# First batch of a windowed attention in blocks of 64 queries by 96 keys, with a joint softmax for its last 64 tokens

## The chip, the cores and the metric

The kernel runs on one core of one Trainium2 chip. The metric is the time of one execution on the device in microseconds (us). Before the change the median of three runs is 910.67 us (910.56 to 910.86).

## What is computed

Attention over 8 batches of 8 heads, 576 tokens, 64 elements a head, in fp32; heads 0 to 3 look back over 32 tokens, heads 4 to 7 over every fourth of the last 128. The result, as 4608 tokens of 512 elements, goes through two dense layers with a clamped square between them.

```python
scores = q @ k.T / 8                       # per batch and head, 576 x 576
rel = pos[:, None] - pos[None, :]
mask_plain = (rel >= 0) & (rel < 32)                       # heads 0 to 3
mask_dil = (rel >= 0) & (rel < 128) & (rel % 4 == 0)       # heads 4 to 7
attn = exp(where(mask, scores, -1e9) - max)
attn = attn / (attn.sum(-1) + 1e-09)
x = (attn @ v), heads side by side         # 4608 x 512
h = x @ w_in                               # 512 x 2048
g = where(h >= 1, h, where(h <= -1, 0, (h + 1) ** 2 / 4))
out = g @ w_out                            # 2048 x 512
```

The weights arrive as 64-bit floating-point words and are made into pairs of fp32r tiles (a high and a low part) on the chip.

## The kernel before, in words

**The dense layers.** The 4608 tokens form 9 tiles of 512, the 2048 hidden elements 16 blocks of 128: 144 steps, named by `s`. In a step `layer1` (line 658) adds up 12 products of 128x128 by 128x512 in the bank `h0` or `h1` (`A s.c` in the order below, three products for each chunk `c` of 128 input elements: high weight by `xh`, low weight by `xh`, high weight by `xl`). Then come `clamped` (VectorE, `y`), `squared` (ScalarE, `s`), `activated` (VectorE, `j`), `g_high` (ScalarE, `g`), `g_low` (VectorE, `d`), and `layer2` (`B s.m`, 12 products for the four blocks `m` of 128 tokens, in the banks `acc0` to `acc3`, through all 16 steps of a tile). A bank `h` is free for the step after next when `g_low` has read it.

**Attention.** Heads are numbered through all batches, 0 to 63. For a head, queries are cut into 6 tiles of 96, each with a stretch of 128 keys that reaches 32 back; for heads 4 to 7 the tokens are sorted by their remainder by 4, so that every fourth token becomes a neighbour. Heads 0 to 15 (two batches, `n < native`) have their scores made directly in fp32 (`scores`, line 309, one product of 64x96 by 64x128 for a tile, two heads of a pair in turn from the upper and the lower 64 partitions); a product in fp32 shows as two records in the trace, a transpose and a product of the dense layers as one. The steps of a head and their letters: `S` scores (TensorE), `r` scale, mask and minimum in one VectorE instruction (line 288), `e` exponential (ScalarE, line 386 for one tile with the sum beside it, line 383 for a whole head, after `z`, GpSimd's subtraction of the minimum, with `u`, VectorE's sum, behind it), `i` and `R` the inverse of the sum (VectorE), `n` the product with it (GpSimd, or VectorE for heads in `by_vector`), `T` six transposes (TensorE, line 470), `p` copies of the turned weights to SBUF (line 476, ScalarE or VectorE by `kept_by_vector`), `V` the product with the values (line 540, in two parts of three tiles for a pair of heads), `x` and `l` the high and the low part of x (ScalarE line 576, VectorE line 581). As a token tile holds 512 tokens and a batch 576, x of a pair is written in three or four pieces.

**The order.** Up to step 17 every engine's order is written out by hand: `OPENING` (line 46) is a list of such letters with the head or the step behind them, played from left to right; each engine takes its instructions in that order. `W` is a number of spin products on a constant that nobody reads; seven more stand ahead of the first scores. `q`, `k`, `v`, `wi`, `wo` are loads, all on SP's queue; `a`, `b`, `j`, `h`, `l` with a weight's name are the five steps that convert a weight block (ScalarE, ScalarE, VectorE, ScalarE or GpSimd, GpSimd). Since SBUF is full, the first batch's queries, keys, values and weights lie in the places of weight blocks that are loaded later (`home`), and its turned weights in the places of the third token tile's x (`first_pts`). From step 18 on a plain loop sets TensorE's and SP's order and a planner the rest.

The opening thus works off the first batch's eight heads, starts the dense layers as soon as x of the first 512 tokens is there, and lays the second batch's heads (8 to 15) among the steps of token tile 0.

Of the kernel before, what the change touches and what calls it, by code (L numbers as in the profile page):

```python
# [49 lines left out]
e3.5 S4.3 R1 S5.3 T0.1 n1 r4.3 e3.0 r4.0 e2 r4.1 r4.2 r5.3 r5.1 e3.2 r5.0 u2 e3.1 W6 S6.0 bwi0 S7.0 S6.1 S7.1  # L50
i3 S6.2 r5.2 S7.2 e4.3 S6.3 R3 S7.3 i2 jwi0 S6.4 e4.2 n3 S7.4 S6.5 S7.5 e4.0 r6.3 r6.0 e4.1 r6.1 e6.3 r6.2
r7.3 W3 S4.4 e6.1 r7.2 r7.1 e6.2 hwi0 r7.0 R2 e6.0 r6.4 S5.4 S4.5 r6.5 S5.5 e6.4 r7.5 T3.0 wi9 r7.4 e6.5 r4.5
n2 T1.0 v2 r4.4 e5.2 p3.0 T1.1 e4.4 wi4 i6 p1.0 r5.5 wi2 R6 r5.4 e4.5 n6 p1.1 q8 W2 T3.1 e5.0 p0.1 T2.0 e5.3
i4 k10 p3.1 V0.0 e5.5 R4 p2.0 wi5 e5.1 T2.1 n4 e5.4 T6.0 wi3 p2.1 x0.0.0 V0.1 u5 wo2 e7.3 e7.0 wi6 l0.0.0
x0.1.0 lwi0 x0.1.1 e7.1 i5 l0.1.0 W2 V2.0 e7.2 R5 l0.1.1 q10 e7.4 T4.0 n5 e7.5 T4.1 V2.1 p6.0 p4.1 i7 x2.0.0
R7 A0.0 p4.0 n7 l2.0.0 x2.1.0 awi1 T5.0 l2.1.0 T6.1 x2.1.1 T5.1 p5.0 bwi1 wi14 T7.0 l2.1.1 p5.1 p6.1 V4.0 awi2
wi7 jwi1 wo3 V4.1 awo0 p7.0 wo9 x4.0.0 T7.1 A0.1 hwi1 p7.1 wo5 l4.0.0 x4.0.1 x4.1.0 lwi1 S8.0 l4.0.1 x4.1.1
S9.0 bwi2 l4.1.0 S8.1 S9.1 V6.0 l4.1.1 bwo0 v8 jwi2 V6.1 awi3 jwo0 A1.0 x6.0.0 hwi2 x6.1.0 wo11 l6.0.0 x6.0.1
x6.1.1 bwi3 A1.1 l6.1.0 wo4 l6.0.1 A0.2 l6.1.1 jwi3 hwo0 A0.3 wi10 S10.0 S11.0 y0 S10.1 S11.1 S8.2 S9.2 S8.3
# [842 lines left out]
```

## Time and profile before

| what | before |
|---|---|
| median of three runs | 910.67 us |
| span of the profiled execution (the profile gives no other time of it) | 910.2 us |
| TensorE busy in the span (matmuls) | 898.1 us, 99% |
| VectorE, ScalarE, GpSimd busy | 667.8, 489.3, 234.5 us |
| DMA, mean over the span | 81 GB/s |

Times are counted from the first instruction of the profiled execution. PE is TensorE's matmul, PEld its weight load, DVE is VectorE, ACT is ScalarE, POOL is GpSimd, SP is SyncE, whose queue issues the loads. Matmuls are pipelined, so durations of single ones overlap, and the distance between starts tells their price. In a row of a stage, the numbers behind its length are the busy time (and instructions) of TensorE's matmuls, its weight loads, VectorE, ScalarE and GpSimd, or of the one engine asked for, then the granted clock of TensorE (1.00 is 2.4 GHz), the DMA engines' busy share and GB/s. The page cuts the span into 40 slices: DMA is busy for over 80% of the first three (68 us) and for 10 to 30% later, and TensorE is at 90% or more in all but the first and the last.

### The profile page before, as it was taken

How to read it: one execution, taken by the hardware profiler on the slowest of the kernel's cores; microseconds unless marked ns; L12 is line 12 of the kernel's file. 1: busy time of each engine (PE TensorE's matmuls, PEld its weight loads, DVE VectorE, ACT ScalarE, POOL GpSimd, SP SyncE). 2: the span in 40 equal slices, each digit the busy share in tenths (PEclk: the TensorE clock that was granted, in tenths of full speed). 3: DMA queues.
4: the chain of work that ended last, by engine and by line, in shares of the span. 5: the costliest groups of instructions: out<-in, count | busy, mean ns of one | idle time of the engine just before them, and what ended most of it. 6: DMA issues, size and time to landing. Idle time of an engine off the chain costs nothing.

```text
span 910.2 us, 14483 instructions
## 1 busy us (share of the span) xinstructions
PE 898.1 (99%) x4855; PEld 739.9 (81%) x4855; DVE 667.8 (73%) x1982; ACT 489.3 (54%) x1402; POOL 234.5 (26%) x163
## 2 busy tenths in 40 slices
PE   8999999999999999999999999999999999999998
PEld 7777887888888888888888888888888888888886
DVE  6897888888888888788888888788888643334333
ACT  7899865545555555555655555555545422223222
POOL 4665571313222212232231322221223000000000
PEclk9999999999999999999999999999999999999999
DMA  8991112212321223222221232222321010001001
GB/s 284 401 381 50 49 37 80 78 59 71 99 90 58 66 64 118 72 71 72 76 84 57 71 104 85 60 70 59 118 71 45 1 47 1 1 0 48 1 1 46
DMA packets 31258, 73.86 MB, mean 81 GB/s; under 512 B 3568, under 2 KB 4432, under 8 KB 31184
## 3 DMA queue, kind: packets, MB, share of 16 engines
q1 hardware_dynamic: 30928, 72.66, 24.4%
q8 instruction: 38, 0.62, 0.3%
q14 instruction: 36, 0.29, 0.1%
q10 hardware_dynamic: 256, 0.28, 0.1%
HBM read 63.49 MB, written 9.44 MB: 80 GB/s over the span
## 4 chain that ended last, share of the span: by engine, by line
PE 69%; DVE 12%; ACT 8%; POOL 6%; issue 3%; DMA 1%; SPq 0%; ACTq 0%; DVEq 0%; POOLq 0%
PE h L670 32%; PE acc L726 32%; POOL kk L253 3%; DVE thirds L434 3%; ACT c L386 2%; PE s L336 2%; POOL c L423 2%; DVE gl L697 2%; PE o L628 2%; DVE pt L434 2%; ACT kk L245 1%; ACT y L683 1%; ACT qs L242 1%; DVE c L360 1%; DVE y L680 1%
## 5 line engine op out<-in xcount | busy, mean ns | idle before, releaser
L726 PE MATMUL acc<-wo,gh 128*128 128x512 f32 x1150 | 383.9, 391 | 0.0
L670 PE MATMUL h<-xh,wi 128*128 128x512 f32 x1152 | 358.7, 393 | 1.4 <-DVE gl L697 1.4
L726 PEld LDWEIGHTS acc<-wo,gh 128*128 128x128 f32 x1150 | 216.1, 188 | 44.0
L670 PEld LDWEIGHTS h<-xh,wi 128*128 128x128 f32 x1152 | 208.0, 188 | 40.8 <-DVE gl L697 1.1
L670 PE MATMUL h<-xl,wi 128*128 128x512 f32 x576 | 224.4, 390 | 0.0
L726 PE MATMUL acc<-wo,gl 128*128 128x512 f32 x575 | 224.1, 390 | 0.0
L386 ACT ACTIVATE c<-c 96x128 f32<-96x128 f32 x330 | 128.3, 393 | 128.0 <-DVE c L288 128.0
L683 ACT ACTIVATE y<-y,consts 128x512 f32<-128x512 f32 x144 | 104.2, 724 | 169.3 <-DVE y L680 168.3
L253 POOL TENSOR_TENSOR kk<-kr,kk 128x608 fp32r<-128x608 f32 x48 | 89.0, 1855 | 408.3 <-ACT kk L245 399.7
L686 DVE TENSOR_TENSOR h<-h,y 128x512 f32<-128x512 f32 x144 | 100.6, 699 | 67.1 <-ACT y L683 66.3
L697 DVE TENSOR_TENSOR gl<-h,gh 128x512 fp32r<-128x512 f32 x144 | 99.0, 687 | 50.6 <-ACT gh L693 49.6
L680 DVE TENSOR_SCALAR y<-h 128x512 f32<-128x512 f32 x144 | 98.4, 683 | 48.2 <-PE h L670 47.8
L693 ACT CAST gh<-h 128x512 fp32r<-128x512 f32 x144 | 84.2, 585 | 91.3 <-PE acc L726 76.1
L670 PEld LDWEIGHTS h<-xl,wi 128*128 128x128 f32 x576 | 108.2, 188 | 23.3
L726 PEld LDWEIGHTS acc<-wo,gl 128*128 128x128 f32 x575 | 108.0, 188 | 20.5 <-DVE gl L697 0.2
L423 POOL TENSOR_TENSOR c<-c 96x768 f32<-96x768 f32 x51 | 74.8, 1466 | 28.5 <-DVE c L418 27.9
L288 DVE CUSTOM_DVE_ANT_0 c<-s,c 96x128 f32<-96x128 f32 x288 | 71.0, 280 | 1.1
L360 DVE TENSOR_TENSOR c<-s,fixed 96x256 f32<-96x256 f32 (+1 forms) x168 | 61.3, 376 | 11.2 <-PE s L336 9.6
L386 ACT ACTIVATION_READ_ACCUMULATOR c<-c 96x1 f32 x318 | 59.7, 188 | 0.0
L434 DVE STREAM_TRANSPOSE thirds<-c 32x192 f32<-32x192 f32 x144 | 53.1, 369 | 8.5 <-POOL c L423 6.9
L336 PEld LDWEIGHTS s<-kk,qs 128*96 128x96 f32 x288 | 46.4, 161 | 15.4
L336 PE MATMUL s<-kk,qs 128*96 128x256 f32 x288 | 57.7, 283 | 0.0
(90 smaller groups left out, 675.4 us busy)
## 6 DMA issues: line engine op xcount, KB each, us to landing
kr<-k_in SPq DMA_DIRECT2D x52, 304.0 KB, 3.2
qr<-q_in SPq DMA_DIRECT2D x52, 288.0 KB, 2.8
vt<-v_in SPq DMA_DIRECT2D x29, 384.0 KB, 3.9
out<-out SPq DMA_DIRECT2D x35, 256.0 KB, 3.2
wi_raw<-w_in SPq DMA_DIRECT2D x16, 512.0 KB, 8.8
wo_raw<-w_in SPq DMA_DIRECT2D x16, 512.0 KB, 9.7
v_place<-v_in SPq DMA_DIRECT2D x3, 384.0 KB, 9.7
k_place<-k_in SPq DMA_DIRECT2D x3, 304.0 KB, 5.4
```

What stands on the lines that cost most here:

```text
L253: nc.gpsimd.tensor_tensor(out=kk[:, 1], in0=kr, in1=kk[:, 0].bitcast(F32), op=ALU.subtract)
L336: PE.matmul(out=split_view(n, t0)[:, t - t0], lhsT=hd["qs"][:, t * QT : (t + 1) * QT], rhs=hd["ks"][:, :, t * QT : t * QT + 128], start=Tr ...
L386: nc.scalar.activation(out=c[:, t], in_=c[:, t], func=AF.Exp, bias=st[:, 0, t : t + 1], scale=-1.0, **total)
L423: engine.tensor_tensor(out=c, in0=c, in1=spread(factor(n)), op=ALU.mult)
L434: nc.vector.transpose(out=pt_of(n)[r : r + 32, :, 32 * g : 32 * g + 32], in_=heads[n]["c"][32 * g : 32 * g + 32, :, r : r + 32],)
L670: PE.matmul(out=hps[s], lhsT=ready[f"wi{f}"][:, w, 128 * c : 128 * c + 128], rhs=x[:, c], start=c == 0 and i == 0, stop=c == NC - 1 and i ...
L680: nc.vector.tensor_scalar(out=y, in0=hps[s], scalar1=-1.0, scalar2=1.0, op0=ALU.max, op1=ALU.min)
L683: nc.scalar.activation(out=ys[s], in_=ys[s], func=AF.Square, bias=half_t, scale=0.5)
L686: nc.vector.tensor_tensor(out=hps[s], in0=hps[s], in1=ys.pop(s), op=ALU.max)
L693: nc.scalar.copy(out=gs[s][0], in_=hps[s])
L697: nc.vector.tensor_tensor(out=gl, in0=hps.pop(s), in1=gh.bitcast(F32), op=ALU.subtract)
L726: PE.matmul(out=acc[m], lhsT=g[:, r], rhs=w[:, part], start=f == 0 and i == 0, stop=(f == NF - 1 or s == len(steps) - 2 and m == TOK // 12 ...
```

## The change

The first batch's heads (0 to 7) get functions of their own; heads 8 to 63 are computed as before.

- Queries of a head are cut into blocks of 64 with 96 keys each, eight of them for the first 512 tokens. `scores_block` writes two blocks at a time, one on the upper and one on the lower 64 partitions of the bank, for both heads of a pair: four products that use the four quarters of the array. A tile of `c` then has 128 rows (two blocks) by 96 keys, and a head four tiles instead of six.
- Transposes are four per head, of 128 columns; one copy of 512 columns keeps the turned weights. The values product has 16 products of 64 columns for a pair, whose output is one bank of 512 tokens in the order of the token tile, and x of a pair is written in one piece (`x`, `l` without numbers).
- The last 64 tokens of the eight heads go through one joint softmax on a tile of 128 rows by 4 x 96 (`tail_...`): scores into two banks, a minimum for each head, then one instruction each for subtraction, exponential, sum, inverse and product, four transposes, one copy, twelve products with the values, and one `x` and `l` for token tile 1. These lie among the steps of token tile 0.
- Of the exponentials, six heads' are whole passes after GpSimd's subtraction (`z`), two heads' (0 and 2) by tile.
- New inputs (`qb`, `kb`, `vb`, `vbt`, `block_in`) hold the first batch in this layout; the loads, the places in `home` and the banks (`PLACES`) are set anew, and the masks of the first batch come in two pieces, the 96x128 masks of the other heads later.
- `OPENING` is written anew: the first score product stands behind 19 spin products instead of 7 (26 in all before and after), and the order of all loads, conversions and of the second batch's heads differs. GpSimd makes 16 of the 32 high weight parts instead of 18. The loop from step 18 on is the same.

The order of three engines, as the built programs have it. In the names, `c` holds the weights of a head, `t` is a bank with turned weights, `o` one with the values product, `s` scores, `pts` the turned weights in SBUF, `h` a bank of layer 1, and `place` a borrowed tile.

ScalarE in the kernel before, from its fourth group of exponentials on.

```order
L386 ACTIVATE c_99<-c_99 96x128 x4
L202 ACTIVATE thirds<-wi_raw 128x512
L386 ACTIVATE c_place<-c_place 96x128 x4
L383 ACTIVATE c_place<-c_place 96x768
L386 ACTIVATE c_place<-c_place 96x128 x2
L208 ACTIVATE wi_raw<-wi_raw 128x512
L386 ACTIVATE c_place<-c_place 96x128 x12
L476 COPY pts_xh<-t_0_315 128x384
```

And ScalarE from its first exponential on with the change.

```order
L438 ACTIVATE c_107<-c_107 128x96 x4
L435 ACTIVATE c_107<-c_107 128x384
L438 ACTIVATE c_151<-c_151 128x96 x2
L435 ACTIVATE c_151<-c_151 128x384
L530 COPY pts_xh<-t_212 96x512
L438 ACTIVATE c_151<-c_151 128x96
L229 ACTIVATE thirds<-wi_raw 128x512
L235 ACTIVATE wi_raw<-wi_raw 128x512
```

Most exponentials of single tiles have become whole passes of 384 elements, and ScalarE's first copy of turned weights comes after eight exponential instructions instead of 31.

TensorE around the first layer-1 products of step 0 before.

```order
L670 MATMUL h_0_191<-xh_386,wi_291 128x512 x2
L670 MATMUL h_0_191<-xl_387,wi_291 128x512
L470 MATMUL t_0_457<-fixed,c_place 128x96 x4
L470 MATMUL t_4_463<-fixed,c_place 128x96 x2
L470 MATMUL t_4_467<-fixed,c_place 128x96 x2
L470 MATMUL t_0_474<-fixed,c_place 128x96 x4
L540 MATMUL o_0_482<-pts_xl,v_place 64x96 x6
L540 MATMUL o_1_495<-pts_xl,v_place 64x96 x6
```

And with the change (`tsa` and `tsb` are the tail's score banks).

```order
L520 MATMUL t_319<-tc_place,c_151 96x128 x4
L520 MATMUL t_324<-tc_place,c_151 96x128 x4
L560 MATMUL o_336<-pts_xh,v_place 64x64 x16
L560 MATMUL o_360<-pts_xh,v_place 64x64 x16
L520 MATMUL t_388<-tc_place,c_place 96x128 x4
L629 MATMUL tsa<-k_place,q_place 32x96 x2
L629 MATMUL tsb<-k_place,q_place 32x96 x2
L798 MATMUL h_0_77<-xh_379,wi_330 128x512 x2
L798 MATMUL h_0_77<-xl_380,wi_330 128x512
L520 MATMUL t_408<-tc_place,c_place 96x128 x4
L520 MATMUL t_414<-tc_place,c_place 96x128 x4
```

The first chunk of layer 1 stands behind the values of two pairs in both; the groups around it are now one row of 16 products or of four transposes, and the tail's scores stand among them.

VectorE at the first low parts of x before.

```order
L581 TENSOR_TENSOR xl_387<-o_0_360,xh_386 128x288
L410 TENSOR_SCALAR sums<-c_place 96x6
L581 TENSOR_TENSOR xl_387<-o_1_389,xh_386 128x224
L418 RECIPROCAL c_place<-sums 96x6
L581 TENSOR_TENSOR xl_407<-o_1_389,xh_406 128x64
L476 COPY pts_xl<-t_4_434 128x192
```

And with the change.

```order
L530 COPY pts_xh<-t_319 96x512
L640 ISA tc_place<-tsb,tc_place 64x96
L640 ISA tc_place 64x1
L448 TENSOR_REDUCE c_place<-c_place 128x4 x2
L461 TENSOR_SCALAR sums<-c_place 128x4 x2
L469 RECIPROCAL c_place<-sums 128x4 x2
L613 TENSOR_TENSOR xl_380<-o_336,xh_379 128x512
L448 TENSOR_REDUCE c_place<-c_place 128x4
```

Three pieces of x have become one of 512 columns; sums of whole heads and the tail's minima (line 640) are new in the queue.

The diff, cut to its core:

```diff
+BQ, BK, NB = 64, 96, 8
+TAIL = NB * BQ
...
-q0 k0 msk K0 Q0 q2 k2 q4 mk2 S0.0 S1.0 S0.1 S1.1 k4 S0.2 S1.2 r0.0 wi0 r0.1 e0.0 r0.2 r1.2 e0.1 r1.0 S0.3 r1.1
...
+q0 W7 k0 Q0 K0 msk W6 q2 k2 W6 S0.0 W2 q4 k4 k6 mk1 q6 S0.1 S0.3 S0.2 wi0 wi1 v0 r0.1 r0.3 r0.2 r1.2 r0.0 r1.0 r1.3
+r1.1 S2.0 e0.3 e0.2 S2.1 S2.3 S2.2 e0.1 e0.0 u0 z1 i0 R0 S4.0 n0 r3.3 r3.2 r3.0 r3.1 r2.2 r2.1 e1 wi2 v2 S4.2 S4.1
...
+    def load_tail():
+        tail["v"] = borrow("tv")[:BK, : 12 * D]
+        nc.sync.dma_start(out=tail["v"], in_=vbt)
...
-    cast_by_pool = ('wo0', 'wi2', 'wi3', 'wo2', 'wi12', 'wi0', 'wo11', 'wi13', 'wo1', 'wo12', 'wo15', 'wi10', 'wi8', 'wo14', 'wo8', 'wo6', 'wi6', 'wi15')
+    cast_by_pool = ('wi2', 'wo1', 'wi3', 'wi4', 'wo2', 'wi6', 'wi8', 'wo7', 'wi10', 'wo10', 'wi12', 'wi13', 'wi15', 'wi14', 'wo15', 'wo14')
...
-            if n == t0 == 0:
-                spin(7, scored[n, t0])
+            scored[n, t0] = bank(f"s{n}_{t0}")
...
+    def scores_block(n, t):
+        if n not in scored:
+            for j in range(2):
+                scored[n + j] = bank(f"s{n + j}")
+        for half in range(2):
+            first = 2 * BQ * t + BQ * half if n < H // 2 else (CLS + 32) * t + BQ * half
+            for j in range(2):
+                r = slice(64 * j, 64 * j + 64)
+                PE.matmul(
+                    out=scored[n + j][BQ * half : BQ * (half + 1), BK * t : BK * (t + 1)],
+                    lhsT=whole["q", n][r, BQ * (2 * t + half) : BQ * (2 * t + half + 1)],
+                    rhs=whole["k", n][r, first : first + BK],
+                    start=True,
+                    stop=True,
+                )
...
+        if n < H:
+            kind = 0 if t == 0 or n >= H // 2 else 1
+            reduce(n, t, (scored[n][:, BK * t : BK * (t + 1)], bmsk()[:, kind]))
...
-    whole_pass = (2, 11)
-    sum_apart = (5, 9, 14, 15)
-    by_vector = (8, 11, 12, 13, 14, 15)
+    sum_apart = (0, 5, 9, 14, 15)
+    by_vector = (8, 11, 12, 13, 14, 15, 16)
...
-    kept_by_vector = {(0, 1), (12, 1), (7, 1), (2, 1), (0, 0), (3, 1), (6, 1), (1, 1), (7, 0), (2, 0), (12, 0), (3, 0), (14, 0), (5, 0), (9, 1), (4, 1)}
-
+    def transpose_pe(n, half=None):
+        c = heads[n]["c"]
+        if n < H:
+            tp = turned_pe[n] = bank(f"t{n}")
+            for t in range(NB // 2):
+                PE.transpose(tp[:BK, 2 * BQ * t : 2 * BQ * (t + 1)], c[:, t], bident())
+            return
...
+    def kept(n, half=None):
+        if n < H:
+            copy = nc.vector.tensor_copy if n in kept_by_vector else nc.scalar.copy
+            copy(out=pt_of(n), in_=turned_pe.pop(n)[:BK])
+            return
...
+    def weighted(n, part=None):
+        if n < H:
+            op = valued[n] = bank(f"o{n}")
+            for t in range(NB):
+                cols = slice(BQ * t, BQ * (t + 1))
+                for j in range(2):
+                    o = op[64 * j : 64 * j + 64]
+                    if n < H // 2:
+                        o = o[:, cols]
+                    else:
+                        o = o.rearrange("p (i r) -> p r i", r=DIL)[:, t // 2, BQ * (t % 2) : BQ * (t % 2 + 1)]
+                    PE.matmul(
+                        out=o, lhsT=heads[n + j]["vt"][:, t], rhs=pt_of(n + j)[:, cols], start=True, stop=True
+                    )
...
+    def parts(n, part, piece):
+        if part is None:
+            return valued[n], 0, lambda x: x
+        return pieces(n, part)[piece]
...
+    def x_high(n, part=None, piece=None):
+        src, t, place = parts(n, part, piece)
...
+    def tail_scores(n):
+        if "s" not in tail:
+            tail["s"] = [bank("tsa"), bank("tsb")]
+        at = BK * (n // 2)
+        for j in range(2):
+            r = slice(64 * j, 64 * j + 64)
+            q0, k0 = whole["q", n][r, TAIL:], whole["k", n][r]
+            o = tail["s"][j][:, at : at + BK]
+            if n < H // 2:
+                PE.matmul(out=o[r], lhsT=q0, rhs=k0[:, TAIL : TAIL + BK], start=True, stop=True)
+                continue
+            k0 = k0.rearrange("p (c i) -> p c i", c=DIL)[:, :, 128:]
+            for w in range(2):
+                PE.matmul(
+                    out=o[64 * j + 32 * w : 64 * j + 32 * w + 32].rearrange("p (c i) -> p c i", c=2),
+                    lhsT=q0[:, 32 * w : 32 * w + 32],
+                    rhs=k0[:, 2 * w : 2 * w + 2],
+                    start=True,
+                    stop=True,
+                )
+    def tail_lowest(n):
+        j, t = n % 2, n // 2
+        r = slice(64 * j, 64 * j + 64)
+        nc.vector.tensor_tensor_reduce(
+            out=tail_c()[r, t],
+            in0=tail["s"][j][r, BK * t : BK * (t + 1)],
+            in1=bmsk()[r, 1 if n < H // 2 else 2],
+            scale=-1.0 / 8.0,
+            scalar=3.0e38,
+            op0=ALU.add,
+            op1=ALU.min,
+            accum_out=tail_st(0)[r, t : t + 1],
+        )
+    def tail_shifted():
+        c = tail_c()
+        nc.gpsimd.tensor_tensor(out=c, in0=c, in1=spread(tail_st(0), c), op=ALU.subtract)
+    def tail_exp():
+        nc.scalar.activation(out=tail_c(), in_=tail_c(), func=AF.Exp, scale=-1.0)
+    def tail_summed():
+        nc.vector.tensor_reduce(out=tail_st(1), in_=tail_c(), op=ALU.add, axis=mybir.AxisListType.X)
...
+    def tail_transposed():
+        tail["t"] = bank("tt")
+        for t in range(H // 2):
+            PE.transpose(tail["t"][:BK, 128 * t : 128 * (t + 1)], tail_c()[:, t], bident())
+    def tail_kept():
+        tail["p"] = pts[0].rearrange("p t j -> p (t j)")[:BK, :TOK]
+        nc.scalar.copy(out=tail["p"], in_=tail["t"][:BK])
+    def tail_weighted():
+        tail["o"] = bank("to")
+        at = 0
+        for n in range(0, H, 2):
+            for j in range(2):
+                o = tail["o"][64 * j : 64 * j + 64, BQ * (n // 2) : BQ * (n // 2 + 1)]
+                p = tail["p"][:, BQ * (n + j) : BQ * (n + j + 1)]
+                if n < H // 2:
+                    PE.matmul(out=o, lhsT=tail["v"][:, at : at + D], rhs=p, start=True, stop=True)
+                    at += D
+                    continue
+                o = o.rearrange("p (i r) -> p r i", r=DIL)
+                p = p.rearrange("p (r i) -> p r i", r=DIL)
+                for w in range(2):
+                    two = slice(2 * w, 2 * w + 2)
+                    PE.matmul(out=o[:, two], lhsT=tail["v"][:, at : at + D], rhs=p[:, two], start=True, stop=True)
+                    at += D
...
-            nc.scalar.dma_start(out=fixed[:QT, : 3 * 128], in_=fixed_in[:, : 3 * 128])
+            nc.scalar.dma_start(out=tail_place()[:, : 2 * BK], in_=block_in[:, : 2 * BK])
+        elif token == "mk1":
+            nc.sync.dma_start(out=tail_place()[:, 2 * BK : 3 * BK + 128], in_=block_in[:, 2 * BK :])
         elif token == "mk2":
```

## Rows read from the trace of the kernel before

**Rows 1.** The profile's page, first line.

```profile
span 910.2 us, 14483 instructions
```

**Rows 2.** Busy time by stage: from:to, length, engines (instructions), granted clock, DMA.

```profile
5.48:37.48 32.00, 28.55 (x294) 23.51 (x294) 26.03 (x145) 28.40 (x108) 19.83 (x16) 0.95 0.96 360
...
41.83:100.00 58.17, 56.99 (x353) 45.54 (x354) 49.04 (x132) 53.91 (x142) 34.32 (x29) 1.00 0.55 206
```

**Rows 3.** Waits of TensorE from 45 to 200 us: sum, times, longest.

```profile
PE o L540 <- ACT pt L476: 1.2, 2, 0.6
PE h L670 <- DVE gl L697: 0.9, 1, 0.9
```

**Rows 4.** VectorE in order of time: start, duration, line, operation, tiles.

```profile
5.70 0.28 DVE L288 CUSTOM_DVE_ANT_0 c<-s,fixed 96x128 f32<-96x128 f32 x1
...
5.91 0.28 DVE L288 CUSTOM_DVE_ANT_0 c<-s,fixed 96x128 f32<-96x128 f32 x1
...
36.03 0.86 DVE L581 TENSOR_TENSOR xl<-o,xh 128x256 fp32r<-128x256 f32 x3 [0.37 <-ACT xh L576]
```

**Rows 5.** TensorE in order of time, up to step 2 (x counts records).

```profile
0.92 3.36 PE L273 MATMUL s<-consts 128*128 128x128 f32 x14 [0.92 <-DVE consts L802]
...
14.43 1.53 PE L273 MATMUL h<-consts 128*128 128x128 f32 x12
...
37.09 0.39 PE L670 MATMUL h<-xl,wi 128*128 128x512 f32 x1
37.41 1.55 PE L321 MATMUL s<-kr,qr 64*96 64x128 f32 x24
...
41.83 0.70 PE L670 MATMUL h<-xh,wi 128*128 128x512 f32 x2 [0.46 <-DVE gl L697]
```

**Rows 6.** TensorE in order of time, later: transposes, values, one step's layer 1.

```profile
50.24 0.72 PE L470 MATMUL t<-fixed,c_place 96*128 96x96 f32 x6
...
52.85 1.27 PE L540 MATMUL o<-pt,vt 128*64 128x96 f32 x24
...
56.24 0.62 PE L670 MATMUL h<-xh,wi 128*128 128x512 f32 x2
...
58.96 0.39 PE L726 MATMUL acc<-wo,gh 128*128 128x512 f32 x1
```

**Rows 7.** Busy time by stage, VectorE alone.

```profile
5.48:10.07 4.59, 2.70 (x24) 0.81 1.04 397
10.07:36.89 26.82, 22.74 (x121) 0.97 0.95 353
```

**Rows 8.** VectorE's groups by shape, 5.4 to 37 us: busy, mean ns, idle.

```profile
L396 DVE TENSOR_REDUCE c_place<-c_place 96x6 f32<-96x768 f32 x2 | 1.9, 942 | 0.0
...
L476 DVE COPY pts_xl<-t 128x384 f32<-128x384 f32 x2 | 1.1, 554 | 0.3 <-PE t L470 0.3
...
L476 DVE COPY pts_xl<-t 128x192 f32<-128x192 f32 x2 | 0.7, 352 | 0.9 <-PE t L470 0.9
```

**Rows 9.** Busy time of VectorE's copies of turned weights (line 476).

```profile
5.48:36.89 31.41, 5.10 (x12) 0.95 0.96 359
```

**Rows 10.** Busy time of VectorE's low parts of x (line 581).

```profile
5.48:36.89 31.41, 5.12 (x14) 0.95 0.96 359
```

**Rows 11.** ScalarE's groups by shape, 5.4 to 37 us.

```profile
L386 ACT ACTIVATE c_place<-c_place 96x128 f32<-96x128 f32 x30 | 11.2, 392 | 1.0 <-DVE c_place L288 1.0
L386 ACT ACTIVATE c<-c 96x128 f32<-96x128 f32 x12 | 4.7, 390 | 3.4 <-DVE c L288 3.3
...
L383 ACT ACTIVATE c_place<-c_place 96x768 f32<-96x768 f32 x1 | 0.8, 827 | 0.0
```

**Rows 12.** TensorE's weight loads by shape, 0 to 60 us: one group.

```profile
L540 PEld LDWEIGHTS o<-pts_xl,v_place 128*64 128x64 f32 x36 | 2.1, 136 | 0.1
```

**Rows 13.** Busy time by stage, TensorE alone, around the drop of its clock.

```profile
7.00:8.00 1.00, 0.58 (x12) 1.00 1.06 389
...
9.00:10.00 1.00, 1.00 (x13) 0.50 1.05 409
```

More of the change, by code (lines that the diff above doesn't have):

```diff
@@ L50 @@
[L50 to L59, printed above, removed]
@@ L583, in runs, with tail_views, tail_high, tail_low @@
+    def tail_views():
+        src = tail["o"][:, : BQ * NC].rearrange("p (c j) -> p c j", c=NC)
+        return src, *(x[:, :, :BQ] for x in xtile(1))
+    def tail_high():
+        src, xh, _ = tail_views()
+        nc.scalar.copy(out=xh, in_=src)
+    def tail_low():
+        src, xh, xl = tail_views()
+        nc.vector.tensor_tensor(out=xl, in0=src, in1=xh.bitcast(F32), op=ALU.subtract)
     def runs(n, first, last):
@@ L765, in play @@
             kind = token.rstrip("0123456789.")
-            operations[kind](*(int(x) for x in token[len(kind) :].split(".")))
+            operations[kind](*(int(x) for x in token[len(kind) :].split(".") if x))
     slots = {}
@@ new lines, with classes @@
+    v_in = np.ascontiguousarray(v_in).reshape((B - 1) * H // 2, 128, 2 * NQ * D)
+    def classes(a, axis):
+        a = a.reshape(*a.shape[:axis], CLS, DIL, *a.shape[axis + 1 :])
+        return np.moveaxis(a, axis + 1, axis)
+    q0, k0, v0 = (np.array(a[0]) for a in (q, k, v))
+    near, far = slice(0, H // 2), slice(H // 2, H)
+    front = CLS - 16
+    qd, kd, vd = (classes(a[far], 1) for a in (q0, k0, v0))
+    qd = np.concatenate([qd[:, :, :front].reshape(H // 2, TAIL, D), qd[:, :, front:].reshape(H // 2, S - TAIL, D)], axis=1)
@@ new lines @@
+    qb = np.concatenate([q0[near], qd]).transpose(0, 2, 1).reshape(H // 2, 2 * D, S)
+    before = ((0, 0), (0, 0), (32, 0), (0, 0))
+    kd, vd = np.pad(kd, before), np.pad(vd, before)
+    kn, vn = (np.pad(a[near], ((0, 0), (32, 0), (0, 0))) for a in (k0, v0))
+    wide = np.pad(kn, ((0, 0), (0, DIL * (CLS + 32) - KPAD), (0, 0)))
+    kb = np.concatenate([wide, kd.reshape(H // 2, -1, D)]).transpose(0, 2, 1).reshape(H // 2, 2 * D, -1)
+    window = np.arange(BK)
+    vb = [vn[:, BQ * n + window] for n in range(NB)], [vd[:, n // 2, BQ * (n % 2) + window] for n in range(NB)]
@@ new lines @@
+    vb = np.concatenate([np.stack(a, axis=1) for a in vb])
+    vb = vb.reshape(H // 2, 2, NB, BK, D).transpose(0, 3, 1, 2, 4).reshape(H // 2, BK, 2 * NB * D)
+    ends = vd[:, :, 32 + CLS - 48 :].reshape(H // 2, 2, BK, D)
+    vbt = [vn[n, TAIL + window] for n in range(H // 2)] + [e for n in range(H // 2) for e in ends[n]]
+    vbt = np.stack(vbt, axis=1).reshape(BK, 12 * D)
+    row, col = np.arange(128)[:, None], np.arange(BK)[None, :]
+    at = row % BQ
+    normal = (col > at) & (col <= at + WIN)
@@ L871 @@
+    begins = normal & ((row >= BQ) | (col >= 32))
+    last = (col // 48 == at // 16 % 2) & (col % 48 > at % 16) & (col % 48 <= at % 16 + WIN)
+    block = [np.where(m, 0.0, NEG).astype(np.float32) for m in (begins, normal, last)]
+    block = np.concatenate([*block, np.eye(128, dtype=np.float32)], axis=1)
+    qb, kb, vb, vbt = (np.ascontiguousarray(a) for a in (qb, kb, vb, vbt))
     query = np.arange(QT)[:, None]
@@ L880 @@
     arrays = {
+        "qb_in": qb,
+        "kb_in": kb,
+        "vb_in": vb,
+        "vbt_in": vbt,
+        "block_in": block,
         "q_in": native(qa),
```

282 lines of the change are left out of this document (137 added, 145 removed), and 8 rows, old and new, of tables (PLACES, home).

## The prediction

> **What bounds the kernel now.** I read the page's busy table first, then the busy time of each engine by stage, then TensorE in order of time, then VectorE and ScalarE in the first 37 us. The reader is to see three things. Over the span of 910.2 us [rows 1] TensorE is the engine that hardly rests, so that only two things can shorten the kernel: less TensorE work, or less time in which TensorE is kept from the large products of the two layers. From 41.83 us on TensorE works almost without a break (56.99 of 58.17 us up to 100 us) [rows 2]; up to 200 us its waits sum to 1.2 us for ScalarE's copies of the turned weights and 0.9 us for VectorE's `gl` [rows 3]. So the loss sits ahead of 41.83 us: in 5.48 to 37.48 us ScalarE is busy for 28.40 of 32.00 us, VectorE for 26.03, and TensorE's 28.55 hold spin products [rows 2]. The first batch's softmax, on ScalarE and VectorE, sets when x of the first token tile is complete: VectorE's last `xl` ends at 36.03 + 0.86 = 36.89 us [rows 4], layer 1 of step 0 at 37.09 + 0.39 = 37.48 us, and after a stretch filled with scores of the next batch step 2 begins at 41.83 us [rows 5].
>
> The last 2866 rows of TensorE's order read alike in both kernels; they begin near the end of step 17, some 145 us in, so the result is settled before that: whatever is won at 41.83 us stays won unless a new wait eats it. (About 0.2%, 1.8 us, is what a measurement of this kernel can tell from no change.) The sum is made against the profiled execution, 910.2 us in its span; the median of the three runs shown is 0.47 us above.
>
> **The start is later.** The kernel has 26 spin products before and after, but 19 instead of 7 now stand ahead of the first score product. A product shows as two records. The first 14 records took 3.36 us from 0.92 us on, 0.24 us each; 12 later ones, from 14.43 us on, took 1.53 us, 0.128 each [rows 5]. The 24 added records take 3.1 us at the quick rate and 5.8 us at the slow one, after 0.92 + 3.36 = 4.3 us, and the first score product starts at 7.4 or at 10.1 us. I take 8.2 us, nearer the quick end, since the engine is then already in continuous work. This delays the start by about 4 us.
>
> **TensorE's share of the first batch.** Scores of a pair become 16 products of 64 queries by 96 keys, 32 records, instead of 12. Before, 24 records of 128 columns took 1.55 us, 0.065 each, with two 64-row halves in turn [rows 5]. The new ones lie in four quarters of the array: with no more overlap 0.065 us, with twice the overlap and three quarters of the columns 0.024. The values product goes from 24 records of 96 columns, 1.27/24 = 0.053 us [rows 6], to 32 of 64: 0.053 if set by issue, 0.035 by columns. I take 0.035 for both (the scores' nearest row is that of the products that split the columns too): 1.1 us for each, per pair. Transposes go from six of 96 columns, 0.72 us [rows 6], to four of 128, 0.64 us a head. Twelve layer-1 products took 58.96 - 56.24 = 2.72 us, 0.227 each [rows 6]. From the first score product to the end of step 0's layer 1 stand four pairs of scores (4.5), of values (4.5), eight heads of transposes (5.1), 24 records of the joint tail's scores (0.8), 14 of spins (1.8), 18 layer-1 products (4.1): 20.8 us, to 29.0 us at the earliest. With the slow prices (0.065, 0.053) it is 27.7 us, to 35.9.
>
> **VectorE's queue.** Its busy time from 5.48 to 36.89 us was 2.70 + 22.74 = 25.4 us [rows 7]. The steps of its masked minimum follow at 0.21 us (5.70, 5.91) [rows 4]. An element costs (554 - 352)/192 = 1.05 ns [rows 8], so a step on 96 keys takes 0.177 us.
> - 48 minima leave (-10.1), 32 for the blocks and 8 for the tail come (+7.1).
> - Sums in a pass of their own: two of 768 elements at 0.94 us [rows 8] become seven of 384 at about 0.5: +1.6.
> - Copies of turned weights: 12, 5.10 us [rows 9], become two of 512 columns at 0.55 + 0.13 = 0.69: -3.7.
> - `xl`: 14 pieces, 5.12 us [rows 10], become four at 0.69: -2.4.
> Left are 17.9 us. The queue can begin when the second block's scores stand, 8.2 + 16 x 0.035 + two spins (0.5) + 0.2 = 9.5 us. Its idle share in 10.07 to 36.89 us was 4.08 of 26.82, 15% [rows 7], nearly all waits on TensorE and ScalarE, which stay; 17.9 us become 20.6, and the last `xl` ends at 30.1 us, above TensorE's 29.0. Step 0's layer 1 ends 0.6 us behind, as it did: 30.7 instead of 37.48 us.
>
> **ScalarE and GpSimd lie beside it.** 30 + 12 exponentials of one tile in that stretch (0.39 us each) [rows 11] become 8, with six whole passes of 384 elements at less than the 0.83 of 768 [rows 11]; at 0.39 and 0.5 that is -13.3 + 3.0, and 28.4 us go to about 18 within 22 us: it stops being the bound. GpSimd gains six passes that subtract the minimum and loses half of every pass's length: no more work than before.
>
> **Transfers** were at 0.96 of their share in that stage [rows 2]; the masks move behind the fourth pair's keys, the tail's values (288 KB) come in ahead of the fourth weight block, under 1 us at 360 GB/s. On SP's queue one block waits for the last turned pair, with three behind it, one being step 2's second-layer weights; those are read twenty microseconds later: nothing.
>
> **From there on.** Between layer 1 of step 0 and step 2 there were 4.35 us, set by the chain over VectorE and ScalarE [rows 5]. Now 40 records of scores (2.6), two chunks of layer 1 (1.4) and the tail's transposes (0.6) stand there: 4.6 us, so step 2 begins at 35.3 instead of 41.83, 6.5 us earlier. The tail's values product, 24 records, comes later at 0.053: -1.3, between 0.8 and 1.3. The rest of TensorE's work up to the common order is the same products. 6.5 - 1.3 = 5.2 us: 905.0 in the span, **905.5 us** for the median. Weight blocks already converted at the end of step 0's layer 1 number five in both.
>
> **Rivals.**
> 1. *Better* (chance 0.13): VectorE's idle time shrinks to half and the two later waits (2.1 us) vanish since batch 1's copies are reordered: 1.3 + 2.1 more, 902.1. For: ScalarE, which VectorE waited for, is freed. Against: TensorE's 29.0 us is close behind.
> 2. *ScalarE gives it back* (0.15): from 41.83 to 100 us it is busy for 53.91 of 58.17 us [rows 2], 93%. The tail adds an exponential pass, a small step, a copy and a cast (at most 0.83 + 0.2 + 0.7 + 0.7), and two more weight casts fall to it (0.7 each): 3.8 us in the place of TensorE's 1.3. 908.0. Against: TensorE hardly waited there.
> 3. *Weight loads bind* (0.14). The loads for the values product, of 64 columns, show 136 ns each [rows 12]. If two at a time is the most the quarters allow, a record of scores takes 0.068 us: (128 + 24) x 0.033 = 5.0 us more on TensorE, which then binds: 8.2 + 25.8 = 34.0 instead of 30.7, 908.8. [...]
> 4. *Slower: the clock drops* (0.10). In 7 to 8 us TensorE was busy for 0.58 us, and in 9 to 10 us its granted clock was 0.50, the 1.2 GHz level [rows 13]. The spins that stood at 14.43 us are now ahead, and between 9 and 22 us TensorE waits for VectorE and GpSimd between short groups. If the clock is low there, scores (4.5), four heads of transposes (2.6), two pairs of values (2.2) and the tail's (0.8) double: 10.1 us on a path with 1.1 us of room (30.1 against 29.0), 914.5. It decides from about 6 us of such work at half clock. Against: the work is denser than before.
>
> **How the numbers follow.** The forecast has 0.48, the rivals 0.13, 0.15, 0.14 and 0.10. Its own range: start -0.8 to +1.9, VectorE's idle 0 to twice (-2.7, +2.7), tail's product -0.5, later waits -2.1 to +2.1; taken as independent, -3.6 to +3.9, 901.9 to 909.4. The range 901.9 to 909.6 takes in rivals 1 to 3 and leaves out rival 4 and some tails. Faster by over 0.2% (under 908.85): 0.47 + 0.13 + 0.12 + 0.07 = 0.79. Within 0.2%: 0.01 + 0.03 + 0.06 + 0.01 = 0.11. Slower: 0.01 + 0.09 = 0.10.
>
> **What would show it.** First score product at 8.2 us; score records at 0.035 us apart; VectorE's last `xl` of step 0 near 30 us with ScalarE under 90% busy before it; step 2's layer 1 near 35 us; TensorE without breaks from there; a granted clock of 1.00 from 10 us on. The forecast is wrong if step 2 begins after 38 us, if TensorE waits for more than 4 us between there and 150 us, or if a record of scores takes over 0.06 us.

## The result and the profile after

The changed kernel takes 920.31 us (median of 4 runs, 919.63 to 920.55), the kernel before, run beside it, 910.76 us (910.56 to 911.09). The ratio is 1.0103 with a 95% interval of 1.0089 to 1.0117: slower by 1%, where 905.5 us was forecast. The profiled execution took 920.14 us.

The opening went much as forecast. TensorE in order of time up to step 2, from the trace of the changed kernel:

```profile
7.42 0.40 PE L371 MATMUL s<-kr,qr 64*64 64x96 f32 x8
...
8.94 1.50 PE L371 MATMUL s<-k_place,q_place 64*64 64x96 f32 x64
12.85 0.64 PE L520 MATMUL t<-tc_place,c 128*96 128x128 f32 x4 [2.41 <-POOL c L474]
...
19.99 2.08 PE L560 MATMUL o<-pts_xh,v_place 96*64 96x64 f32 x64
...
31.51 0.39 PE L798 MATMUL h<-xl,wi 128*128 128x512 f32 x1
31.83 0.67 PE L354 MATMUL s<-kr,qr 64*96 64x128 f32 x4
33.41 2.72 PE L354 MATMUL s<-kr,qr 64*96 64x128 f32 x36 [0.91 <-DMA qr<-q_in]
...
37.92 0.71 PE L798 MATMUL h<-xh,wi 128*128 128x512 f32 x2
```

The first score product starts at 7.42 us, step 0's layer 1 ends at 31.51 + 0.39 = 31.90 us, and step 2 begins at 37.92 us: 3.9 us earlier than in [rows 5]. Busy time by stage, to be set beside [rows 2], shows where that goes (engines PE, PEld, DVE, ACT, POOL with their instructions, then the granted clock, the DMA share and GB/s):

```profile
16.00:32.00 16.00, 14.71 (x204) 11.25 (x203) 15.18 (x60) 13.52 (x28) 13.19 (x14) 1.00 1.04 267
37.92:100.00 62.08, 59.36 (x354) 46.62 (x353) 48.16 (x125) 51.80 (x137) 33.44 (x27) 0.97 0.63 241
50.00:60.00 10.00, 8.25 (x31) 6.02 (x30) 6.99 (x14) 6.45 (x16) 8.45 (x5) 0.83 0.91 320
100.00:120.00 20.00, 18.49 (x110) 14.35 (x105) 18.37 (x47) 15.73 (x35) 13.89 (x12) 1.00 0.11 32
...
150.00:160.00 10.00, 5.82 (x20) 4.49 (x19) 8.44 (x22) 3.21 (x9) 1.46 (x1) 0.83 0.59 205
```

TensorE now stands still for 1.75 us in 50 to 60 us, 1.51 us in 100 to 120 us and 4.18 us in 150 to 160 us, and in the first and the last of these stretches its clock is granted at 0.83 on the mean. The waits of TensorE from 38 to 165 us name the causes; before there were 1.4 us for `gl` and 1.2 us for a copy in the same stretch ([rows 3] has them from 45 us on).

```profile
PE h L798 <- DVE gl L825: 5.7, 2, 4.2
PE acc L854 <- POOL wo L247: 1.1, 1, 1.1
PE acc L854 <- POOL wo L251: 0.6, 1, 0.6
PE t L525 <- DVE c L474: 0.6, 1, 0.6
```

In order of time, TensorE around the first and the last of them:

```profile
55.01 0.50 PE L854 MATMUL acc<-wo,gh 128*128 128x512 f32 x1 [1.13 <-POOL wo L247]
55.35 0.40 PE L854 MATMUL acc<-wo,gl 128*128 128x512 f32 x1
56.37 1.14 PE L854 MATMUL acc<-wo,gh 128*128 128x512 f32 x2 [0.63 <-POOL wo L251]
57.31 0.63 PE L854 MATMUL acc<-wo,gl 128*128 128x512 f32 x1
...
155.46 1.22 PE L798 MATMUL h<-xh,wi 128*128 128x512 f32 x2 [4.18 <-DVE gl L825]
156.47 0.63 PE L798 MATMUL h<-xl,wi 128*128 128x512 f32 x1
```

A record of 512 columns that took 0.39 us takes 0.63 us behind both waits. The granted clock (third number from the end) is there at 0.52 in 57 to 60 us and at 0.50 in 156 to 158.5 us, as a share of full speed; no run shows it in GHz. Taken at 0.50 for as long as it is low, the means of 0.83 make that some 3.4 us (10 x 0.17 / 0.5) in each of the two stretches of 10 us, an estimate, and less than the expectations below have it:

```profile
57.00:60.00 3.00, 3.00 (x11) 2.35 (x10) 0.96 (x2) 1.03 (x4) 1.79 (x2) 0.52 1.00 396
156.00:158.50 2.50, 2.50 (x7) 1.97 (x6) 2.37 (x7) 0.00 (x0) 0.00 (x0) 0.50 0.60 228
```

What TensorE waits for stands late in another engine's queue. GpSimd's two passes on block wo2 (`hwo2`, `lwo2`) stand behind head 11's subtraction, which took 3.42 us where a product of the same size took 1.47; and VectorE comes to step 16's `gl` (154.71) only behind two copies of outputs, five turns of weights (`STREAM_TRANSPOSE`), a reciprocal and step 17's maximum:

```profile
48.48 1.47 POOL L474 TENSOR_TENSOR c_place<-c_place 96x768 f32<-96x768 f32 x1 [0.26 <-DVE c_place L469]
50.26 3.42 POOL L444 TENSOR_TENSOR c<-c 96x768 f32<-96x768 f32 x1 [0.31 <-DVE c L323]
53.62 1.33 POOL L247 CAST wo<-thirds 128x512 fp32r<-128x512 f32 x1
```

```profile
150.40 1.37 DVE L866 COPY out<-acc 128x512 f32<-128x512 f32 x2 [0.85 <-PE acc L854]
151.80 0.37 DVE L485 STREAM_TRANSPOSE pt<-c 32x192 f32<-32x192 f32 x1
152.20 0.19 DVE L469 RECIPROCAL c<-c 96x6 f32<-96x6 f32 x1
152.41 1.14 DVE L485 STREAM_TRANSPOSE pt<-c 32x192 f32<-32x192 f32 x3
153.58 0.70 DVE L814 TENSOR_TENSOR h<-h,y 128x512 f32<-128x512 f32 x1
154.31 0.37 DVE L485 STREAM_TRANSPOSE pt<-c 32x192 f32<-32x192 f32 x1
154.71 0.69 DVE L825 TENSOR_TENSOR gl<-h,gh 128x512 fp32r<-128x512 f32 x1
```

A second thing stands in the rows by stage: the DMA engines are as full as before (1.04), but move 267 GB/s in 16 to 32 us, where the whole stretch of [rows 2] had 360 and these 16 us of the kernel before 335.

### The profile page after: what moved, and what is told of

Same layout as the page of the kernel before. It is cut to its first block, busy times and chain, and to the rows that moved or that the text cites. A ratio compares the mean times of both kernels' runs of the same rounds, so it can differ in the third digit from the quotient of the medians.

```text
span 918.4 us, 14567 instructions
## 1 busy us (share of the span) xinstructions
PE 898.3 (98%) x4955; PEld 738.9 (80%) x4955; DVE 667.8 (73%) x1956; ACT 481.0 (52%) x1338; POOL 234.0 (25%) x167
## 4 chain that ended last, share of the span: by engine, by line
PE 68%; DVE 12%; ACT 8%; POOL 6%; DMA 3%; issue 3%; SPq 0%; ACTq 0%; DVEq 0%; POOLq 0%
PE acc L854 31%; PE h L798 31%; POOL kk L280 3%; DVE thirds L485 3%; ACT c L438 2%; PE s L386 2%; POOL c L474 2%; DVE gl L825 2%; PE o L756 2%; DMA v_place<-vb_in 2%; DVE pt L485 2%; ACT kk L272 1%; ACT y L811 1%; ACT qs L269 1%; DVE c L410 1%
## 5 line engine op out<-in xcount | busy, mean ns | idle before, releaser
L438 ACT ACTIVATE c<-c 96x128 f32<-96x128 f32 (+1 forms) x326 | 126.7, 392 | 132.7 <-DVE c L323 132.7
L474 POOL TENSOR_TENSOR c<-c 96x768 f32<-96x768 f32 (+1 forms) x52 | 74.1, 1426 | 21.7 <-DVE c L469 21.0
L438 ACT ACTIVATION_READ_ACCUMULATOR c<-c 96x1 f32 (+1 forms) x310 | 58.2, 188 | 0.0
```

The costliest lines, as they stand in the source:

```text
L438: nc.scalar.activation(out=c[:, t], in_=c[:, t], func=AF.Exp, bias=st[:, 0, t : t + 1], scale=-1.0, **total)
L474: engine.tensor_tensor(out=c, in0=c, in1=spread(factor(n), c), op=ALU.mult)
```

## The experiments

The theories at the start: **1**, each of the three waits costs its own time, and moving the late instruction wins it back; **2**, transfers that arrive late set the pace. Each run was timed beside the kernel before, whose median was 910.8 us for the result above, 911.5 us for the first four runs (single waits and rows), 911.7 for the next six and 911.0 for the last two. Where runs of different groups are compared, the difference against the kernel before is given as well.

**Single waits.** Step 16's `gl` first (the table `OPENING`; the lines show what moved):

```diff
-B14.3 d15 ... j16 m17.2 A17.1 cq18 e17.4 cl18 r17.3 A17.2 ... B15.2 B14.0 B15.0 ... t16.2.0 g16 g17 d16
+B14.3 B14.0 d15 ... j16 m17.2 A17.1 cq18 e17.4 g16 cl18 r17.3 A17.2 d16 ... B15.2 B15.0 ... t16.2.0 g17
```

> In the profile of the changed kernel TensorE waits 4.18 us at 151 us for VectorE's gl of step 16, which stands on VectorE behind four turns of the last batch, two output copies and step 17's maximum, and whose gh stands on ScalarE behind step 17's square and two output copies; behind the wait the clock is at half for some 4.5 us. This kernel orders B14.0, g16 and d16 ahead of them and changes nothing else. Theory 1 (the order of work around each wait costs its own time): the wait of 4.18 us and the half clock go, 4 to 6 us, so 914.3 to 916.3 us. Theory 2 (weights and inputs that arrive late set the pace, a wait removed comes back at the next place): within 1 us of 920.3 us.

919.91 us (918.3 to 921.34), no gain clear of the noise. The wait for `gl` is gone from its place; the profile's TensorE waits almost as long some 4 us later, ahead of the next head's scores, for a minimum in VectorE's queue:

```profile
159.50 0.45 PE L383 MATMUL s<-kk,qs 128*96 128x256 f32 x2 [3.76 <-DVE c L320]
```

Block wo2 first:

```diff
-r10.4 z11 awo3 hwi5 e10.4 e10.0 e11 A3.3 ... hwo2 jwo3 n8 lwo2 hwo3
+r10.4 awo3 hwi5 e10.4 e10.0 A3.3 ... hwo2 jwo3 n8 lwo2 z11 hwo3 e11
```

> TensorE waits 1.13 and 0.63 us at 54 to 56 us for GpSimd's two passes on weight block wo2, which stand in GpSimd's queue behind a subtraction of head 11 that took 3.42 us, and its clock is at half from 55 to 60 us. This kernel orders the subtraction (and ScalarE's exponential behind it) after the two passes, nothing else. Theory 1 (order): the waits (1.8 us) and the half clock (2 us or more) go, 916.3 to 918.5 us. Theory 2 (late transfers): the wait comes back at the next block, within 1 us of 920.3 us.

922.44 us (921.56 to 922.65), no gain: 10.9 us above the kernel before, the changed kernel 9.6. The wait for wo2 shrank from 1.7 to 0.5 us, and a new one of 1.9 us came: head 11's exponential, now later, holds up VectorE's queue and with it a copy of turned weights.

```profile
PE h L797 <- DVE gl L824: 5.7, 2, 4.2
PE t L524 <- DVE pt L534: 1.9, 1, 1.9
PE acc L853 <- POOL wo L250: 0.5, 1, 0.5
```

Both, and step 11's `gh` and `gl` ahead of three passes on weights and a minimum (`g11` behind `A12.3`, `d11` behind `e15.3`):

> Both moves of the two kernels before, and in step 11 ScalarE's gh and VectorE's gl put ahead of three passes on weights and a minimum (TensorE waits 1.51 us for that gl at 117 us). Theory 1: the three gains add up, 4 to 6, 2 to 4 and 1 to 1.5 us, so 909 to 913 us, about the kernel before (910.7), and TensorE waits for less than 2 us between 42 and 160 us. Theory 2: little over the better of the two moves, above 915 us.

921.59 us (918.95 to 923.05). The three gains don't add up to anything. Theory 1 falls as I had put it: in these three runs the instruction that was moved ahead pushed back another that TensorE needed next.

**The transfers of 96 rows.**

```diff
-vt = whole["v", n] = borrow(f"v{n}")[:BK]
-nc.sync.dma_start(out=vt, in_=vb[n // 2])
+full = borrow(f"v{n}")
+nc.sync.dma_start(out=full, in_=vb[n // 2])
+vt = whole["v", n] = full[:BK]
...
+vb = np.pad(vb, ((0, 0), (0, 128 - BK), (0, 0)))
+vbt = np.pad(vbt, ((0, 128 - BK), (0, 0)))
```

> The five transfers of the first batch's values have 96 rows; while they are in flight, from 13 to 32.5 us, every transfer's packets are slow (some 65 ns for each KB instead of 40) in the profile of the changed kernel. Here they are padded to 128 rows (a third more bytes, 0.6 MB in all), nothing else. Theory 2a (the 96 rows make the transfers slow): packets at 40 ns for each KB in 14 to 32 us, the weights land some 5 us earlier, step 2 begins about 1 us earlier than 37.92 us, and the whole is 1 to 4 us faster, 916 to 919 us. Theory 1 (order; the slow transfers come from something else or cost little): packets as slow as before, the whole within 1 us of 920.3 us or slower by the added bytes.

917.86 us (917.39 to 918.44). The DMA engines move 386 GB/s in 16 to 32 us, where they moved 267, although the values' transfers carry a third more bytes; busy time by stage of this kernel:

```profile
8.00:16.00 8.00, 5.82 (x140) 4.56 (x138) 5.67 (x51) 4.05 (x14) 3.69 (x5) 0.87 1.03 407
16.00:32.00 16.00, 15.10 (x210) 12.09 (x207) 15.20 (x64) 14.12 (x29) 13.20 (x15) 0.96 1.04 386
```

So the 96 rows cost about 2.4 us (3.2 us against the kernel before: 9.55 us above it became 6.34), and theory 2 holds for that much. But TensorE's waits from 38 us on are the same to a tenth as in the changed kernel, with data that came earlier:

```profile
PE h L800 <- DVE gl L827: 5.7, 2, 4.2
PE acc L856 <- POOL wo L249: 1.1, 1, 1.1
PE acc L856 <- POOL wo L253: 0.6, 1, 0.6
PE t L527 <- DVE c L476: 0.6, 1, 0.6
```

By what way the slow transfers cost time is not shown. In the two profiles step 2 begins only 0.33 us apart (37.92 and 37.59 us); 1.6 us more come between the first products of step 4 and step 5 (51.00 to 62.66 us against 50.64 to 60.73), where both kernels have the same two waits, but the clock is at 0.83 in 50 to 60 us in the changed kernel and at 1.00 in this one.

**Keys of head 14 later.** On SP's queue they wait from 40 to 49.6 us for scores of heads 10 and 11, with weight blocks behind them:

```diff
-wi6 k14 wo6 wi8 v8 wo11 wo7 wi13 wo10 q14 v10
+wi6 wo6 wi8 v8 wo11 wo7 wi13 wo10 k14 q14 v10
```

> The changed kernel with 128 rows, and on SP's queue the keys of head 14 (which wait until 49.6 us for the scores of heads 10 and 11, with the DMA queues empty from about 46 us) moved behind six weight blocks and one block of values. Theory 2 (late transfers): the blocks land up to 8 us earlier, and the whole is 1 to 4 us below 917.9 us. Theories 3 and 4: TensorE's three waits stand, within 1 us of 917.9 us.

918.22 us (918.19 to 920.64): no gain, though the DMA engines moved 397 GB/s in 42 to 50 us where the kernel without this edit moved 211. Late transfers of these blocks are not what holds TensorE up after 42 us.

**The order as a whole.** New theories: **3**, the rearranged order between step 2 and step 17 loses what the opening won, as one; **4**, VectorE and ScalarE are too full there, in any order. The edit keeps the changed kernel's table up to the first product of step 2 and takes that of the kernel before from there on (the grafted kernel below). The old choice of engines for some weight copies and for head 16's product goes with it, so the run tests order and choice together:

```diff
-cast_by_pool = ('wi2', 'wo1', 'wi3', 'wi4', 'wo2', 'wi6', 'wi8', 'wo7', ...)
-by_vector = (8, 11, 12, 13, 14, 15, 16)
+cast_by_pool = ('wi2', 'wi3', 'wo2', 'wi12', 'wo11', 'wi13', 'wo1', 'wo12', ...)
+by_vector = (8, 11, 12, 13, 14, 15)
-tT A2.0 e8.5 awi4 A2.1 y1 r11.0 r9.4 r9.5 r8.1 A2.2 s1 ...
+tT A2.0 y1 r9.5 jwi3 r8.1 tp hwi3 r8.2 e8.0 wi6 wo5 wi8 v8 r9.2 e8.2 r9.3 r9.1 r8.3 e9.0 lwi3 ...
```

> The changed kernel with its transfers padded to 128 rows, its order kept up to the first product of step 2, and from there on the order of the kernel before (with the tail's steps, and the few steps that are left of batch 1, put in; the choice of engine for the weight copies as before, head 16's product with the reciprocals back on GpSimd). Theory 3 (the rearranged order between step 2 and step 17 loses what the opening won): step 2 begins near 38 us as in the changed kernel, TensorE waits for less than 3 us from there to 160 us, and the whole is 907 to 910 us, the opening's 3.9 us less the 1.3 us of the tail's product ahead of the kernel before. Theory 4 (VectorE and ScalarE have too much left to do between 42 and 160 us when the layers start earlier, whatever the order): waits of 5 us and more come at other places, 914 us or more.

911.51 us (910.8 to 911.9), ratio to the kernel before 0.9996 (0.9987 to 1.0005): 6.35 us less than the same opening with the changed order (6.5 us against the kernel before). The profile of this kernel, TensorE's waits from 38 to 300 us:

```profile
PE h L800 <- DVE gl L827: 2.0, 2, 1.1
PE o L569 <- DVE pt L537: 0.7, 1, 0.7
PE o L569 <- ACT pt L537: 0.6, 1, 0.6
PE t L527 <- issue: 0.4, 1, 0.4
PE o L758 <- DVE gl L827: 0.2, 1, 0.2
```

They sum to 3.9 us against 8.4 (two of 0.2 us aren't shown above), and the spans differ by 916.5 - 909.4 = 7.1 us. Theory 3 holds in that the loss goes with the order, and theory 4 falls: nearly the same instructions, some on another engine, fit in without the long waits. Both figures of theory 3 were missed: the waits are 3.9 us instead of under 3, and the time is 1.5 us above its window, so less of the opening's gain is left at the end than I had thought (below). What the order does alone, without the choice of engines, was not run.

> The same with the transfers of 96 rows as in the changed kernel: the price of the slow transfers with the order of the kernel before. Theory 3: 1 to 4 us above the padded one, 909 to 913 us. Theory 4: as far above the padded one as the changed kernel is above its own padded form (2.4 us).

914.8 us (913.96 to 917.32), 3.3 us over the padded one, above the window that theory 3 gave: the 96 rows cost as much with the old order (2.4 and 3.3 us by two pairs). As theory 4 gave about the same price, this run doesn't decide between the two.

The same cut at step 5 (own order up to `A5.0`, the old one from there):

> The changed kernel with 128 rows (917.9 us) and its own order up to the first product of step 5 (55 us), the order of the kernel before from there on. Of TensorE's three waits, that for block wo2 (53 to 60 us, with the half clock behind it) stays, and those of steps 11 and 16 for VectorE's gl go. Theory 3: the loss is a sum over the places, so 911.5 us plus the first wait's 3 to 4 us, 913.5 to 916 us. Theory 4, or a backlog carried from step 5 on: 917 us or more.

914.75 us (913.96 to 915.03), as theory 3 said: 3.1 us of the order's loss go with the part behind step 5, 3.2 us stay. Its profile still shows the 1.1 and 0.6 us for wo2. It also shows, just behind the cut, a wait of 1.9 us (at 62.88 us, for a product on GpSimd) that neither of the other two kernels has, so how the loss is split between the two stretches is rough.

**Can the grafted kernel be helped?** Step 1's square, maximum and copies ahead of batch 1's exponentials and minima (`s1`, `j1`, `g1`, `d1` each 23 to 29 places up in the list):

> The grafted kernel with 128 rows (order of the kernel before from step 2 on, 911.5 us), with step 1's square, maximum and two copies (ScalarE, VectorE) put ahead of batch 1's exponentials and minima that they stood behind: TensorE waited 1.06 us at 42.6 us for step 1's gl. Theory 3 (with this order what is won by step 2 stays won): 0.8 to 1.3 us faster, 910.2 to 910.7 us. Theory 4 (the engines beside TensorE are full, the wait comes back): within 0.4 us of 911.5 us.

911.52 us, nothing: the wait of 1.06 us for `gl` went, one of 1.1 us for VectorE's minima of batch 1 came at the next product. As in the first three runs.

**The start.** Twelve of the 19 spin products put behind the first scores:

```diff
-q0 W7 k0 Q0 K0 msk W6 q2 k2 W6 S0.0 W2 q4 k4 k6 mk1 q6 S0.1 S0.3 S0.2
+q0 W7 k0 Q0 K0 msk q2 k2 S0.0 W2 q4 k4 k6 mk1 q6 S0.1 S0.3 S0.2 W6
-S2.1 S2.3 S2.2
+S2.1 S2.3 S2.2 W6
```

> The same, and 12 of the 19 spin products ahead of the first score product put behind the scores of the first and of the second pair. The first score product starts near 4.5 instead of 7.4 us. If the start is on the path to step 2 and the clock holds, step 2 begins 2 to 3 us earlier and the whole is 907.5 to 909 us; if the clock falls to half without the spins, as it did at 9 to 10 us in the kernel before, the scores and turns lose what the start wins and the whole is within 1 us of the kernel without this change, or slower.

909.67 us (909.42 to 911.89), 0.9981 (0.9972 to 0.9990) of the kernel before: the one version here that is faster than both kernels, by 0.2% against the kernel before, though 0.7 us above the window expected. In its profile step 2 begins 2.4 us earlier than without the edit (37.25), and the granted clock is 1.00 on the mean of the whole execution. The first products of step 2 and step 4:

```profile
34.82 0.71 PE L800 MATMUL h<-xh,wi 128*128 128x512 f32 x2
...
53.04 0.62 PE L800 MATMUL h<-xh,wi 128*128 128x512 f32 x2
```

The same edit in the changed kernel with 128 rows and its own order:

> The changed kernel with 128 rows and its own order throughout (917.9 us), and 12 of the 19 spin products ahead put behind the first scores, as in the grafted kernel, where this won 1.85 us. If the rearranged order loses a fixed sum in waits behind one another, the start's gain stays: 915.5 to 916.5 us. If its waits are for work of other engines that ends at a fixed time (VectorE, ScalarE, GpSimd and the transfers full between step 2 and step 17), TensorE only waits longer: 917 to 918.5 us.

915.44 us (915.26 to 916.89), 2.4 us below 917.86 (1.9 us against the kernel before): the gain stays. And TensorE's waits from 38 us on are once more 5.7, 1.1, 0.6 and 0.6 us, although step 2 begins at 34.91 instead of 37.59 us. So they are not waits for something that ends at a fixed time; they belong to the order.

A last single move in the grafted kernel with seven spin products ahead:

> The grafted kernel with 128 rows and seven spin products ahead (909.7 us), with VectorE's three minima of head 9 that stood behind step 1's maximum and last pass put ahead of them: the first product of layer 2 waited 1.07 us at 37.8 us for the last of them (its bank held head 9's scores). Theory 3 (what is won by step 3 stays won): 0.5 to 1 us faster, 908.7 to 909.2 us. Theory 4: within 0.3 us of 909.7 us, the wait comes back behind step 1's gl, which these minima now delay.

910.46 us (909.62 to 911.74), within its interval no better than 909.67: VectorE's minima moved ahead (`r9.2 r9.3 r9.1` ahead of `j1`) win nothing. In its profile the wait of 1.07 us is gone, and one of 1.47 us stands ahead of the tail's product with the values, for another minimum on VectorE.

## Why the prediction was wrong

**The steps of the opening** held. First score product 7.42 us (forecast 8.2; the quick end of my bounds). Score records 1.50/64 = 0.023 us and values records 2.08/64 = 0.033 (0.035 each): the scores overlap as well as the better bound had it, so rival 3 (weight loads bind) did not happen: the 0.068 us a record that it set did not come. VectorE's queue ended at 30.87 us (30.1), which is partly luck: its busy time was 20.6 us instead of 17.9, and its idle time 1.1 us instead of 2.7. The sum had slipped there too, since waits of 4.08 us that "stay" would have made 17.9 us into 22.0, not 20.6. Step 0's layer 1 ended at 31.90 us (30.7), 5.6 of the 6.8 us forecast. "GpSimd lies beside it" was wrong in the small: TensorE waited 2.41 us at 12.85 for its first normalised weights, and 4.4 us for GpSimd in all from 8 to 32 us.

**"Transfers ... under 1 us"** was the first wrong term. I counted bytes at the old rate. The values came in 96 rows, and with them in flight the rate fell to 267 GB/s; I had nothing in the trace of before that showed a transfer of 96 rows, and should have bounded it. It cost 2.4 to 3.3 us in all. Part of it may show in the wait of 0.91 us at 33.41 for the next batch's queries, which is not there with 128 rows (nor, though, in the grafted kernel with 96); with scores of 36.06 - 31.83 - 0.91 = 3.32 instead of 2.6 us it pushed step 2 to 37.92 us (35.3).

**"From there on"** was the term that failed. "The rest of TensorE's work up to the common order is the same products" is true and prices nothing: I let the order of 42 to 145 us count as neutral because its products are the same, and looked only for work that the change adds. The rearranged order, with the choice of engines that came with it, lost 6.35 us by the pair of runs above; what the runs show there are TensorE's waits of 5.7, 1.1 and 0.6 us for VectorE and GpSimd and the half clock behind some of them. With the old order the kernel stands at 914.8 us, and without the 96 rows too at 911.5, equal to the kernel before. "Whatever is won at 41.83 us stays won unless a new wait eats it" holds for the spin edit, whose gain came through in either order; in the changed kernel new waits ate the gain and more. My own mark, over 4 us of waiting up to 150 us or step 2 after 38 us, was reached only just: up to 150 us it was 4.1 us, and the longest wait came at 151 us.

**The spins** were priced about right in time, but taken as given: the later start costs 1.85 to 2.4 us of the end. In the grafted kernel without it, with 128 rows, step 2 begins at 34.82 us, as early as I forecast; the whole is still 4.2 us above 905.5. Of the 7.0 us won by then 2.5 are left at the end of the profiled executions (907.7 against 910.2).

The trace shows where most of the other 4.5 go. From step 2 to step 4 this kernel takes 18.2 us (34.82 to 53.04), the kernel before 14.4 (41.83 in [rows 5] to 56.24 in [rows 6]). These 3.8 us hold the tail's product (0.9, where I had 1.3), the wait of 1.07 us, one of 0.36 us, and eight records of scores that took 1.08 instead of 0.61 us; the last 1.0 us lies in short gaps. Behind them the lead lasts: 3.2 us at step 4, 2.9 us at step 23 (175.42 against 178.34 us). So "stays won" failed in the first two steps, where the sum had priced nothing but the tail's product, and held from there on.

**The rivals.** The sign was rival 4's, the mechanism wasn't. In the changed kernel's profile the clock was 1.00 from 8 to 50 us. In seven profiles of kernels with its opening it was 0.81 to 0.87 in 8 to 16 us (0.87 in the rows of the 128-row kernel above), and that costs little there: between the grafted kernel, at 1.00, and its variant with step 1 earlier, at 0.83, which issue the same up to there, the last product of step 0's layer 1 starts 0.4 us later (31.99 against 31.58). It fell later, behind TensorE's own waits (to 0.83 on the mean of 50 to 60 and of 150 to 160 us), though not each time: the same waits for wo2 left it at 1.00 in 50 to 60 us in the kernel with 128 rows. Rival 1 came true in its first half, as VectorE's idle time shrank to 1.1 us, but the busy time that the sum had missed ate that. Rival 2 did not happen: ScalarE was busy for 51.80 of 62.08 us, 83%, less than before.

What stays open: which of the order's moves between steps 2 and 17, or of the choices of engine, makes it worse. The cut at step 5 halves the loss, three single moves don't find it. Nor is it shown why a transfer of 96 rows is slow.

## What to carry to other kernels

When a change is bundled with a new order of the work, price the order by itself: take the old order from the first point where both have done the same work, and run that. A single wait removed from a full in-order queue came back at another place in all five runs that tried it here, so judge an order as a whole. And bound every transfer shape that the old trace does not show, even if its bytes are fewer.
